# Fused squared-ReLU attention and MLP on one core: q and k transposed from the layout of their loads, and an order of TensorE's work that pulls MLP products forward

## The chip, the cores and the metric

The kernel runs on one core of a Trainium2 chip. A core has TensorE (matrix products), VectorE (DVE), ScalarE (ACT), GpSimd (POOL) and SyncE (SP), which run side by side and wait for each other through semaphores, and 16 DMA engines that all queues share. The metric is the device time of one execution in microseconds (us). The time before is 370.96 us, the median of three runs from 370.91 to 371.25.

## The reference

```python
# q, k, v: (8, 12, 448, 64)    w_in: (768, 2048)    w_out: (2048, 768)
scores = matmul(q, k.transpose(0, 1, 3, 2)) / sqrt(64)
attn = maximum(scores, 0.0) ** 2 / 448
y = matmul(attn, v)                                   # (8, 12, 448, 64)
x = y.transpose(0, 2, 1, 3).reshape(3584, 768)
h = x @ w_in
out = (0.5 * h * (1 + erf(h / sqrt(2)))) @ w_out      # (3584, 768), float32
```

There is no softmax: each score is scaled, clipped at zero and squared. The output of attention goes straight through a two-layer MLP with the exact GELU. The kernel computes in bf16 with float32 accumulation.

## The kernel before, in words

Work goes by batch b = 0 to 7, each of 448 tokens and 12 heads. The heads are taken in G = 3 groups of four. For each group there are seven steps i (`NK`) of attention: QK (`fn_qk`, L686) makes scores of a block of 64 keys for four heads with four matmuls on four 64x64 tiles of the array at once, ACT or DVE clips them into `a_sq` (L698, L700), DVE squares them (L707), and after the seven steps AV (L746) multiplies them with v in 28 matmuls. The result, copied to bf16, is `xT`. F1 (L800) multiplies it with `w_in` in 16 products of six matmuls, ACT applies GELU into `h_sb` (L810), and the second layer multiplies with `w_out`: plainly for the first 256 rows (`add_plain`, L1203), and for groups of 256 rows with seven products in place of eight (Strassen's scheme, `add_group`, L1108). F1 of batches 5 to 7 uses the same scheme (`add_blocks`, L942). Sums of weights that the scheme needs are made by DVE (`tsum` from `w_out`, `wsum` from `w_in`). QK and AV use 64-wide tiles of the array, all MLP products 128-wide ones.

QK needs q and k with the 64 values of a head on the partitions. Natural rows are loaded by GpSimd's queue with a cast to bf16, as `nq` (112 partitions, for each head 4 chunks of 64 values) and `nk` (128 partitions, for each pair of heads 7 chunks of 64). For batches 0 and 1, TensorE transposes them (`add_tk`, `add_tq`). From batch 2 on a DMA transpose on SyncE's queue does it (`add_T_dma`, L632 for kT, L641 for qT). A transpose takes blocks of 128 columns, that is two chunks of 64 at a time: the first lands on partitions 0 to 63, the second on 64 to 127. For QK the two must be chunks that belong together (e = 0 and e = 1 of a pair), so the rows are permuted first into `pq` and `pk`. Batch 2 is permuted by DVE (`permute_k`, `permute_q`), batches 3 to 7 by their loads (`add_wide`: 6 DMAs for k, 12 for q, in runs of 64 values, and one for v).

`add_gate` is a small copy on GpSimd that reads what the last transposes of q write. Since GpSimd works in order, loads that stand behind it in `pool_q` wait until the transposes of that batch have landed. For batch 2 the gate stands ahead of two of the three loads of `w_out` (`add_wout(1)`, `add_wout(2)`).

The order of all instructions is made when the kernel is built. Each piece of work is an `Op` with a fixed duration, and `Scheduler.place` plays the engines forward: first the string `ORDER`, a list of the first pieces by engine and number, then for each engine the piece that can start first by these durations. TensorE's pieces from batch 2 on come from a list of their own, `pe_q`: eight F1 products of batch 1 (`LEAD`), then slots of QK steps, an MLP product or AV in the middle and MLP products between. Loads are modelled at a fixed rate from `DMA_FREE` on, a DMA transpose as 1.2 us of SyncE that lands 3.0 us after its start. On the chip every engine keeps this order and waits where the work isn't ready. Of a batch b + 1 the transposes may not start before a given slot of batch b (`at`).

Of the kernel before, what the change touches and what calls it, by code (L numbers as in the profile page):

```python
# [23 lines left out]
FF = 2048  # L24
KD = DM // 128
# [10 lines left out]
T_TWO = 0.72  # L36
# [8 lines left out]
DMA_FREE = 4.54  # L45
# [11 lines left out]
NEAR = 0.5  # L57
# [4 lines left out]
WIDE = 2.0  # L62
# [13 lines left out]
G0 G1 G2 G3 G4 G5 A10 D13 G6 A16 P11 P14 G7 D12 A15 P17 G8 D18 P21 P39 D22 P33 P36 A34 D40  # L76
P19 D20 A37 P23 G9 P42 P48 D24 P54 A43 D35 A49 P51 D44 P25 D38 A52 D41 G117 A55 D53 P45 D50
A26 D47 A46 P57 D56 P69 P66 A58 D70 P27 G118 A67 P29 D59 P63 G119 A28 D71 P60 A64 G120 D68
P78 D61 A62 P75 A79 D65 P81 P31 D30 A76 D80 P96 G121 D32 A97 P72 D77 G122 A82 D98 P129 G123
D74 A73 P90 D130 P84 P108 A91 G124 D83 P131 A85 D109 P93 P141 D132 A94 D92 P102 D95 P105  # L80
P111 A103 D86 P143 D110 G125 A106 D104 P99 A112 D107 G126 A144 P87 D100 A101 D113 A142 P157
P114 D88 G127 A158 D89 P133 D115 A116 G128 P135 D159 A134 P160 P163 D136 P166 A164 P145 D167
A161 D165 P253 A146 D168 D162 P169 P172 G147 A254 P175 A173 D170 P245 G148 A176 D171 P255
A246 D177 G149 D174 P184 P187 A256 P196 A185 G150 D188 P137 P139 A138 P178 D197 G151 A140
D186 P193 P211 G152 D180 P247 A212 G153 D213 P249 A248 D179 A194 D198 G154 P263 A250 D195
D229 G155 P223 P220 A264 D189 P190 S235 A224 D221 P265 G156 A191 D225 P267 A266 D192 D222
P199 P217 A268 P214 D231 A218 P257 S236 D215 A200 D219 P259 A258 D216 D201 P181 P208 A260
P205 D230 A209 P261 D182 P251 D183 A262 D210 A206 D233 P202 A252 S237 D207 D232 P226 D234
A203 D204 S238 S239 P269
# [17 lines left out]
class Scheduler:  # L107
# [151 lines left out]

    def place(self, fixed):  # L260
# [14 lines left out]
        while rest or any(fixed.values()):  # L275
# [7 lines left out]
            for e, v in fixed.items():  # L283
                if v and not (e == "PE" and by.get("PE")):
                    tops.append(self.pick(v[:1]))
# [11 lines left out]
def kernel(  # L297
# [34 lines left out]
    q32 = natpool.tile([KC, 4, HC * D], F32, tag="pq", name="q32")  # L332
    k32 = natpool.tile([128, 2, NK * D], F32, tag="pk", name="k32")

    def get_nat(b):
        if b not in nq:

            tq, tk = ("pq", "pk") if b == 1 else ("nq", "nk")
            nq[b] = natpool.tile([KC, H, NC * D], BF16, tag=tq, name="nq")
            nk[b] = natpool.tile([128, HP, NK * D], BF16, tag=tk, name="nk")  # L340
            vt[b] = vpool.tile([128, HP, NK * D], BF16, tag="v", name="v_sb")

# [4 lines left out]
    def load_q(b, g0, g1, c0=0, c1=NC):  # L347
        get_nat(b)
        nc.gpsimd.dma_start(  # L349
            nq[b][:, 4 * g0 : 4 * g1, c0 * D : c1 * D], q_view(b, g0, g1, c0, c1)  # L350
        )
# [25 lines left out]
    pqk = []  # L377

    def get_p():
        if not pqk:  # L380
            pqk.append(natpool.tile([KC, NC, DM], BF16, tag="pq", name="pq"))
            pqk.append(natpool.tile([128, G, NK * 128], BF16, tag="pk", name="pk"))
        return pqk

# [3 lines left out]
    def get_T(b):  # L388
        if b not in qkT:
            qkT[b] = (  # L390
                tpool.tile([128, HP, S], BF16, tag="qT", name="qT"),
                tpool.tile([128, G, NK * 128], BF16, tag="kT", name="kT"),
            )
        return qkT[b]

# [24 lines left out]
    Pq, Pk, Tq, Tk = {}, {}, {}, {}  # L420
# [3 lines left out]
    def war(b):  # L424

        old = [o for (bb, *_), o in list(Pq.items()) + list(Pk.items()) if bb == b - 1]
        c = {1: -1, 2: 0}.get(b, b - 1)
        old += [o[0] for (bb, *_), o in list(Tq.items()) + list(Tk.items()) if bb == c]
        return old
# [19 lines left out]
    def add_v(b, g0, g1):  # L449
        def fn():  # L450
            get_nat(b)
            nc.gpsimd.dma_start(vt[b][:, 2 * g0 : 2 * g1], kv_view(v, b, g0, g1))  # L452

        old = [o for (bb, *_), o in AV.items() if bb == b - 3]
        o = dma(fn, (g1 - g0) * 4 * S * 256, old)
        for g in range(g0, g1):
            ld_v[b, g] = [o]

    def add_wide(b):


        def k_fn(e):
            def fn():
                to = get_p()[1].rearrange("p g (i e d) -> e p g i d", e=2, d=D)
                src = kv_view(k, b, 0, G).rearrange("p (g e) (i d) -> e p g i d", e=2, d=D)
                for g in range(G):
                    nc.gpsimd.dma_start(to[e][:, g], src[e][:, g])  # L467

            return fn

        def q_fn(e, j):
            def fn():
                to = get_p()[0].rearrange("p c (g j e d) -> j e g p c d", j=2, e=2, d=D)
                src = q[b].rearrange("(g e j) (p c) d -> j e g p c d", e=2, j=2, c=NC)
                for g in range(G):
                    nc.gpsimd.dma_start(to[j][e][g], src[j][e][g])  # L476

            return fn

        def v_fn():  # L480
            vt[b] = vpool.tile([128, HP, NK * D], BF16, tag="v", name="v_sb")
            nc.gpsimd.dma_start(vt[b], kv_view(v, b, 0, G))

        n = G * 4 * S * 256
        ks = [dma(k_fn(e), WIDE * n / 2, war(b), G) for e in range(2)]
        qs = [dma(q_fn(e, j), WIDE * n / 4, war(b), G) for e in range(2) for j in range(2)]
        old = [o for (bb, *_), o in AV.items() if bb == b - 3]
        o = dma(v_fn, n, old)
        ops = Both(ks), Both(qs)
        for g in range(G):  # L490
            ld_v[b, g] = [o]
            Pk[b, g] = ops[0]
            for c in range(NC):
                Pq[b, g, c] = ops[1]

    class Both:


        def __init__(self, ops):
            self.ops = ops  # L500

        @property
        def done(self):
            ends = [o.done for o in self.ops]
            return None if None in ends else max(ends)

    def add_load(b, g0=0, g1=G):
        if b > 2:
            return add_wide(b)
# [16 lines left out]

    def permute_k(copy, g, src):

        copy(
            get_p()[1][:, g].rearrange("p (i e d) -> p e i d", e=2, d=D),  # L530
            src.rearrange("p e (i d) -> p e i d", d=D),
        )

    def permute_q(copy, g, c0, c1, src):

        dst = get_p()[0][:, c0:c1, 256 * g : 256 * g + 256].rearrange(
            "p c (j e d) -> e p j c d", j=2, d=D
        )
        for e in range(2):
            copy(dst[e], src[:, 2 * e : 2 * e + 2].rearrange("p j (c d) -> p j c d", d=D))  # L540

    def add_pk(b, g0, g1, after=(), bias=0.0):
        for g in range(g0, g1):
            deps = ld_k[b, g] + list(after)
            deps += [Tk[max(b - 1, 1), x, i][0] for x in range(G) for i in range(NK)]
            Pk[b, g] = sch.add(
                (("DVE", 0.31, 0.43),),
                lambda e, g=g: permute_k(V.tensor_copy, g, nk[b][:, 2 * g : 2 * g + 2]), deps,
                bias=bias,
            )  # L550

    def add_pq(b, g0, g1, c0=0, c1=NC, after=(), bias=0.0):
        for g in range(g0, g1):
            deps = [ld_q[b, g, c] for c in range(c0, c1)] + list(after)
            deps += [Tq[max(b - 1, 1), g, c][0] for c in range(c0, c1)]
            if b == 2:
                deps += [Tq[1, x, c][0] for x in range(G) for c in range(NC)]
            d = 2 * (0.07 + (c1 - c0) * 128 / 3840)

            def fn(e, g=g):  # L560
                permute_q(
                    V.tensor_copy, g, c0, c1, nq[b][:, 4 * g : 4 * g + 4, c0 * D : c1 * D]
                )

            op = sch.add((("DVE", d, d + 0.12),), fn, deps, bias=bias)
            for c in range(c0, c1):
                Pq[b, g, c] = op
# [31 lines left out]
    def add_tq(b, g, c0=0, c1=NC, bias=T_BIAS):  # L599
# [14 lines left out]
        def fn2(e):  # L614
            copy(e, get_T(b)[0][:, 2 * g : 2 * g + 2, c0 * KC : c1 * KC], box[0])
# [11 lines left out]
    def add_T_dma(b, after):  # L627

        after = [list(x) for x in after]
        for g in range(G):  # L630
            def fn(e, g=g):
                nc.sync.dma_start_transpose(  # L632
                    get_T(b)[1][:, g].rearrange("p (i t) -> p i t", t=128), get_p()[1][:, g]
                )

            op = sch.add((("SP", 1.2, 3.0),), fn, [Pk[b, g]] + old_T(b) + after.pop(0), mode="X")
            for i in range(NK):
                Tk[b, g, i] = (op, op)
        for c in range(NC):
            def fn(e, c=c):  # L640
# [813 lines left out]
```

## Time and profile before

| | |
|---|---|
| time, median of three | 370.96 us |
| span of the profiled execution | 368.9 us |
| TensorE busy | 358.9 us, 3557 matmuls |
| DVE busy | 288.3 us |
| ACT busy | 200.8 us |
| GpSimd busy | 108.0 us, of it 41.8 for q's loads into `pq` and 28.9 for k's into `pk` |
| DMA packets of GpSimd's loads (q0) | 74992, 58.6% of the time of 16 engines |
| DMA packets of SyncE's queue (q1), transposes and stores | 38768, 26.8% |
| DMA transposes | 18 for kT, 6.8 us to landing (median), 24 for qT, 3.8 us |
| granted TensorE clock | 0.999 |

The profile is one execution. "Busy" of an engine counts its instructions, not what issues DMAs or waits on semaphores. The chain is followed back from the last instruction, at each step to what released it; so its lines tell which work set the end. In a timeline line the numbers are start and duration in us, then engine, line, operation, output and input, count, and in brackets the idle time before with what ended it. "SPq" are DMA issues of SyncE's queue. q0 is the queue that GpSimd's DMAs go through, q1 that of SyncE.

### The profile page before, as it was taken

The numbers are of one execution on the slowest core, as the hardware profiler recorded it, in microseconds if no ns is written. First come the engines' busy times: TensorE is split into PE (matmuls) and PEld (weight loads), VectorE is DVE, ScalarE is ACT, GpSimd is POOL, SyncE is SP. The second block draws the span as 40 slices with busy tenths as digits, with TensorE's granted clock in tenths as the row PEclk, the third lists the DMA queues.
The fourth block names the chain that finished last, engine by engine and source line by source line (L and its number), as shares of the span: only waits on it lengthen the run. The fifth ranks groups of instructions, "written<-read, shape, count | busy, mean of one in ns | idle before, by whom it ended". The sixth has DMA issues, their size and how long they took to land.

```text
span 368.9 us, 8544 instructions
## 1 busy us (share of the span) xinstructions
PE 358.9 (97%) x3557; PEld 222.1 (60%) x3557; DVE 288.3 (78%) x493; ACT 200.8 (54%) x308; POOL 108.0 (29%) x149
## 2 busy tenths in 40 slices
PE   8799999999999999999999999999999999999994
PEld 7566645455544455544455545457886897688663
DVE  2998991789868978987699888888998658665862
ACT  4988865664447845677755588853440353044200
POOL 8666401726087096097095000000000000000000
PEclk9999999999999999999999999999999999999999
DMA  9999999999999999999999960003002301310233
GB/s 174 196 200 204 202 189 134 173 171 131 244 135 167 160 85 172 209 163 154 146 93 133 205 117 2 3 0 87 2 0 88 85 2 29 109 36 2 85 85 88
DMA packets 114166, 42.98 MB, mean 116 GB/s; under 512 B 92816, under 2 KB 110672, under 8 KB 114128
## 3 DMA queue, kind: packets, MB, share of 16 engines
q0 software_dynamic: 74992, 22.47, 58.6%
q1 hardware_dynamic: 38768, 19.46, 26.8%
q8 instruction: 28, 0.46, 0.5%
q10 hardware_dynamic: 368, 0.51, 0.4%
q14 instruction: 10, 0.08, 0.1%
HBM read 45.61 MB, written 11.01 MB: 153 GB/s over the span
## 4 chain that ended last, share of the span: by engine, by line
PE 87%; DMA 4%; DVE 4%; ACT 2%; POOL 1%; issue 1%; DVEq 0%; POOLq 0%; ACTq 0%
PE pso L1108 32%; PE psh L800 24%; PE pb L942 13%; PE ps L686 8%; PE pav L746 6%; PE pso L1203 3%; DMA v_sb<-in_v_dram 2%; DVE a_sq L707 2%; DMA nk<-in_k_dram 2%; ACT a_sq L698 2%; POOL nk L434 0%; POOL v_sb L452 0%; POOL nq L349 0%; PE tp L580 0%; DVE a_sq L700 0%
## 5 line engine op out<-in xcount | busy, mean ns | idle before, releaser
L698 ACT ACTIVATE a_sq<-ps 128x896 bf16<-128x896 f32 (+1 forms) x136 | 117.4, 914 | 44.6 <-PE ps L686 44.5
L707 DVE TENSOR_TENSOR a_sq<-a_sq 128x896 bf16<-128x896 bf16 (+1 forms) x169 | 97.5, 617 | 7.5 <-ACT a_sq L698 7.2
L800 PE MATMUL psh<-xT,win_sb 128*128 128x448 bf16 (+1 forms) x516 | 96.6, 340 | 0.1
L800 PEld LDWEIGHTS <-win_sb 128*128 128x128 bf16 x516 | 47.8, 98 | 45.5 <-issue 10.2
L810 ACT ACTIVATE h_sb<-psh 128x448 bf16<-128x448 f32 x80 | 43.9, 549 | 24.1 <-PE psh L800 23.9
L1108 PEld LDWEIGHTS <-s_sb 128*128 128x128 bf16 x424 | 40.6, 98 | 27.0 <-issue 2.2
L700 DVE TENSOR_SCALAR a_sq<-ps 128x896 bf16<-128x896 f32 x33 | 35.9, 1090 | 18.3 <-PE ps L686 17.8
L686 PE MATMUL ps<-qT,kT 64*64 64x448 bf16 (+1 forms) x756 | 47.3, 336 | 2.2 <-ACT qT L402 0.6
L976 DVE TENSOR_TENSOR part<-pb,part 128x448 f32<-128x448 f32 x60 | 34.6, 619 | 18.4 <-PE pb L942 18.4
L476 POOL DMA_DIRECT2D pq<-in_q_dram x60 | 41.8, 704 | 10.1 <-DVE a_sq L707 6.4
L1108 PEld LDWEIGHTS <-h_sb 128*128 128x128 bf16 x312 | 29.9, 98 | 21.1 <-issue 2.5
L1108 PE MATMUL pso<-wout_sb,s_sb 128*128 128x384 bf16 (+2 forms) x216 | 38.1, 320 | 0.3 <-DVE osb L1142 0.3
L1108 PE MATMUL pso<-wout_sb,h_sb 128*128 128x384 bf16 x208 | 38.1, 326 | 0.0
L1108 PE MATMUL pso<-t_sb,s_sb 128*128 128x384 bf16 x208 | 38.1, 326 | 0.0
L746 PE MATMUL pav<-a_sq,v_sb 64*64 64x448 bf16 (+1 forms) x756 | 36.8, 330 | 0.7 <-ACT a_sq L698 0.4
L686 PEld LDWEIGHTS <-kT 64*64 64x64 bf16 x756 | 18.3, 105 | 24.2 <-issue 17.4
L985 ACT ACTIVATE h_sb<-part 128x448 bf16<-128x448 f32 x36 | 19.8, 578 | 19.9 <-DVE part L976 19.8
L467 POOL DMA_DIRECT2D pk<-in_k_dram x30 | 28.9, 966 | 1.5 <-issue 0.9
L746 PEld LDWEIGHTS <-v_sb 64*64 64x64 bf16 x756 | 21.1, 107 | 13.0 <-issue 2.3
L942 PEld LDWEIGHTS <-win_sb 128*128 128x128 bf16 x288 | 27.6, 98 | 2.2 <-issue 0.4
L1142 DVE TENSOR_TENSOR osb<-pso,p_sb 128x384 f32<-128x384 f32 x39 | 21.7, 556 | 8.2 <-PE pso L1108 5.7
L400 DVE CAST xT<-pav 128x448 bf16<-128x448 f32 (+1 forms) x43 | 23.7, 583 | 4.6 <-PE pav L746 3.9
(62 smaller groups left out, 292.0 us busy)
## 6 DMA issues: line engine op xcount, KB each, us to landing
pk<-in_k_dram POOLq DMA_DIRECT2D x30, 112.0 KB, 4.4
pq<-in_q_dram POOLq DMA_DIRECT2D x60, 56.0 KB, 5.0
v_sb<-in_v_dram POOLq DMA_DIRECT2D x5, 672.0 KB, 9.1
out_dram<-osb SPq DMA_DIRECT2D x8, 336.0 KB, 3.0
wout_sb<-in_moe_w_out_dram POOLq DMA_DIRECT2D x2, 1152.0 KB, 12.1
v_sb<-in_v_dram POOLq DMA_DIRECT2D x9, 224.0 KB, 8.8
out_dram<-osb SPq DMA_DIRECT2D x7, 288.0 KB, 3.4
out_dram<-osb SPq DMA_DIRECT2D x8, 240.0 KB, 3.1
```

The source lines that it names most:

```text
L467: nc.gpsimd.dma_start(to[e][:, g], src[e][:, g])
L476: nc.gpsimd.dma_start(to[j][e][g], src[j][e][g])
L686: nc.tensor.matmul(ps[64 * j : 64 * j + 64, e, x * w : x * w + w], kT[r, g, i * 128 + 64 * j : i * 128 + 64 * j + 64], qT[r, 2 * g + j, co ...
L698: A.activation(ar, ps, AF.Relu, scale=c_att)
L700: V.tensor_scalar(ar, ps, c_att, 0.0, op0=mybir.AluOpType.mult, op1=mybir.AluOpType.max,)
L707: V.tensor_mul(box["a2"][:, :, :used], ar, ar)
L746: nc.tensor.matmul(pav[0][o2 : o2 + 64, e, :w], vt[b][r, 2 * g + e, bass.ts(i, D)], box["a2"][r, e, o : o + w], start=(i == 0), stop=(i == ...
L800: nc.tensor.matmul(ph[:, x * n : x * n + n], win_sb[:, kd, bass.ts(m + x, 128)], xT[b][:, kd, c], start=(kd == 0), stop=(kd == KD - 1),)
L810: A.activation(h_ring()[:, m : m + nm, o + c.start : o + c.stop], box[0][:, :S].rearrange("p (x n) -> p x n", x=nm), AF.Gelu,)
L942: nc.tensor.matmul(bank[name][:, y, z * HS : z * HS + HS], w[:, k, bass.ts(mm, 128)], right()[:, k], start=first and k == 0 and z == 0, st ...
L976: V.tensor_add(get(to), ps(name), get(other))
L1108: nc.tensor.matmul(box[bank][:, n0:n1], left()[:, kf], right[:, kf, n0:n1], start=bool(need) and kf == 0, stop=kf == K2 - 1, skip_group_ch ...
```

## The change

The two transposes read `nq` and `nk` as they were loaded. For k a block of 128 columns holds two neighbouring chunks of the same 14 (two heads of seven chunks), so step i with half e takes chunk 2i + e, which may be of the first or the second head; QK and AV index accordingly. For q all 48 chunks of a batch stand in a row. One transpose of the row gives the even chunks on the lower and the odd on the upper half; a second one that starts 64 columns earlier gives the other parity. Both go into alternating places of a `qT` of 49 slots (`SLOTS`), so that each half of the partitions holds all chunks in order. That takes nine transposes a batch (per group of heads one for k, an even and an odd one for q) in place of seven, no copies, and one load each for q, k and v of batches 3 to 7. Two edge columns of `nq` are set to zero. The gate now waits for all q transposes of its batch, and that of batch 2 moves behind `add_wout(1)` and `add_wout(2)`. The buffers `pq` and `pk` go; natural rows of batch 1, the first float32 rows and sums at the end move to other buffers, and `tsum` tiles are made when first used.

In the planner, `pick_pe` is new: where the next piece of TensorE's list would wait longer than `PULL` (or `PULL_IN` between 64-wide pieces), the next MLP product of the list is taken if it can start sooner. `DMA_FREE`, `NEAR` and the modelled times of a transpose change. `ORDER` is the same list without the six permuting copies (D229 to D234), with the numbers after them shifted by four and its five SyncE entries now the first five of the nine transposes.

```diff
-T_TWO = 0.72
-DMA_FREE = 4.54
+DMA_FREE = 3.05
+SLOTS = H * NC + 1
-NEAR = 0.5
+PULL = 0.15
+PULL_IN = 0.45
+NEAR = 0.25
-WIDE = 2.0
+T_STEP = 1.6
+T_TIME = 4.5
...
+    def pick_pe(self, v):
+        top = self.pick(v[:1])
+        wait = math.inf if top is None else top[1] - self.free["PE"]
+        if v[0].mode == "F" or wait <= (PULL if self.mode == "F" else PULL_IN):
+            return top
+        nxt = next((o for o in v if o.mode == "F"), None)
+        other = nxt and self.pick([nxt])
+        if other and other[1] - self.free["PE"] <= PULL and other[1] < self.free["PE"] + wait:
+            return other
+        return top
...
-                    tops.append(self.pick(v[:1]))
+                    tops.append(self.pick_pe(v) if e == "PE" else self.pick(v[:1]))
...
+                nq[b] = natpool.tile([KC, (H * NC + 2) * D], BF16, tag="nq", name="nq")
+                nk[b] = natpool.tile([128, HP, NK * D], BF16, tag="nk", name="nk")
+                nc.gpsimd.memset(nq[b][:, :D], 0.0)
+                nc.gpsimd.memset(nq[b][:, D + H * NC * D :], 0.0)
...
-                tpool.tile([128, HP, S], BF16, tag="qT", name="qT"),
+                tpool.tile([128, SLOTS * KC], BF16, tag="qT", name="qT"),
...
     def add_load(b, g0=0, g1=G):
-        if b > 2:
-            return add_wide(b)
         add_k(b, g0, g1)
         add_q(b, g0, g1)
         add_v(b, g0, g1)
...
+        def turn(dst, src, deps):
+            return sch.add(
+                (("SP", T_STEP, T_TIME),),
+                lambda e: nc.sync.dma_start_transpose(dst(), src()),
+                deps + old_T(b) + after.pop(0), mode="X",
+            )
+        def slots_of(n, o, k):
+            return lambda: get_T(b)[0].rearrange("p (s t) -> p s t", t=KC)[
+                :, 2 * n + o : 2 * (n + k) + o - 1 : 2
+            ]
+        def q_src(n, o, k):
+            return lambda: nq[b][:, 128 * n + D * o : 128 * (n + k) + D * o]
...
+        n0, odd = 0, None
         for g in range(G):
+            op = turn(k_dst(g), k_src(g), list(ld_k[b, g]))
             for i in range(NK):
                 Tk[b, g, i] = (op, op)
+            lands = list(dict.fromkeys(ld_q[b, g, c] for c in range(NC)))
+            n = 8 * g + 9
+            even = turn(slots_of(8 * g, 1, 8), q_src(8 * g, 1, 8), lands)
+            prior = odd or even
+            beyond = [ld_q[b, g + 1, c] for c in range(NC)] if g < G - 1 else []
+            beyond = list(dict.fromkeys(beyond))
+            odd = turn(slots_of(n0, 0, n - n0), q_src(n0, 0, n - n0), lands + beyond)
+            n0 = n
+            for c, o in enumerate((even, odd, prior, odd)):
+                Tq[b, g, c] = (o, o)
...
-            nc.gpsimd.tensor_copy(gate, get_T(b)[0][:, 0, ::KC])
-        deps = [Tq[b, 0, c][0] for c in range(NC)]
+            nc.gpsimd.tensor_copy(gate, get_T(b)[0][:, ::KC])
+        deps = [Tq[b, g, c][0] for g in range(G) for c in range(NC)]
...
+                            if b < 2:
+                                moving = q_rows(b)[r, 2 * g + j, cols(half)]
+                            else:
+                                n = 4 * (4 * g + 2 * ((2 * i + e) // NK) + j) + 1 - e
+                                moving = qT[r, n * KC : n * KC + S]
...
-            for i, x in enumerate(blocks):
-                _, box, o = SQ[x]
+            for i in range(NK):
...
+                        n, y = (i, e) if b < 2 else divmod(NK * e + i, 2)
+                        _, box, o = SQ[blocks[n]]
...
-                            box["a2"][r, e, o : o + w],
+                            box["a2"][r, y, o : o + w],
...
-    for g in range(G):
-        add_pk(2, g, g + 1, bias=T_TWO)
-        add_pq(2, g, g + 1, bias=T_TWO)
-    add_T_dma(2, [[]] * 7)
-    add_gate(2)
+    add_T_dma(2, [[]] * 9)
     add_wout(1)
     add_wout(2)
+    add_gate(2)
...
-            add_T_dma(b + 1, [at(b, n + (y >= 4)) for y in range(7)])
+            add_T_dma(b + 1, [at(b, n + (y >= 5)) for y in range(9)])
```

## The prediction

> **What bounds the kernel now.** I read the page's busy line first, then who waits for whom on TensorE, then the chain, then the queues of SyncE, GpSimd and the DMA rings around the one place where the change can push on TensorE.
>
> ```profile
> PE 358.9 (97%) x3557; PEld 222.1 (60%) x3557; DVE 288.3 (78%) x493; ACT 200.8 (54%) x308; POOL 108.0 (29%) x149
> ```
>
> TensorE is busy 97% of the span, but the page says that the ends of matmuls are modelled, so I check with cadences from the chain: 80 products of 384 columns in 13.00 us (0.163 us each), 48 of 224 columns in 4.60 us (0.096), 18 of 448 columns in 3.40 us (0.189); QK and AV run four tiles at once, 28 matmuls in 1.32 us. Times the counts of the groups (444 x 0.189 + 72 x 0.096 for F1, 784 x 0.163 for the second layer, 504 x 0.096 for the blocks, 2 x (147 x 0.189 + 42 x 0.096) for QK and AV, some 7 us of transposes and short ones) this is about 337 us of pure streaming. The last matmul ends at 364.3 us, the tail after it is 4.6. Taking each stretch of 10 us as its length less the streaming that starts in it, some 14 us are lost before 30 us (the first loads, then ACT and DVE at 9.4 of 10 us), and only about 11 us from 60 to the end, nearly all of it 0.09 us at each change between 64-wide and 128-wide tiles. The wait list of TensorE from 66 us on has one line:
>
> ```profile
> PE pso L1108 <- DVE osb L1142: 0.3, 1, 0.3
> ```
>
> Matmul starts add four gaps of 0.28 us (152, 203, 233, 244 us) and one of 0.5 at 98 us. So there are 1.6 us to be won by filling TensorE's waits, and any new wait on TensorE after 55 us is paid in full. The chain shows the place to look at:
>
> ```profile
> 54.77 10.32 PE psh L800 x54
> 65.09 0.50 PE ps L686 x8
> ```
>
> The 54 matmuls are the last F1 product of batch 0 and the eight products of batch 1 that `LEAD` puts ahead of batch 2; QK of batch 2 starts straight after them at 65.0. What it needs was ready only just before:
>
> ```profile
> 42.96 11.90 SPq L632 DMA_TRANSPOSE kT<-pk  x3
> 54.96 6.94 SPq L641 DMA_TRANSPOSE qT<-pq  x4
> ```
>
> ```profile
> 63.48 0.19 POOL L653 COPY gate<-qT 128x4 bf16<-128x4 bf16 x1 [19.21 <-DMA qT<-pq]
> 63.71 1.65 POOL L372 DMA_DIRECT2D wout_sb<-in_moe_w_out_dram  x2
> ```
>
> The last DMA transpose landed at 63.4, 1.6 us before use. And GpSimd held two thirds of `w_out` (2 x 1152 KB) back behind the gate until then. The landing times of transposes, first the three of kT issued from 42 to 54 us, beside loads, then the four of qT from 120 to 130 us, with hardly any:
>
> ```profile
> DMA to landing us min/median/max: 8.6/9.8/12.0
> ...
> DMA to landing us min/median/max: 2.7/3.1/4.0
> ```
>
> Why: packets of the two DMA queues (q0 GpSimd's loads, q1 SyncE's transposes; packets, MB, share) in 48 to 50, 50 to 52 and 52 to 54 us, and q1 alone in 60 to 62 us:
>
> ```profile
> q0 software_dynamic: 424, 0.25, 87.8%
> q1 hardware_dynamic: 421, 0.11, 46.2%
> ...
> q0 software_dynamic: 325, 0.29, 94.3%
> q1 hardware_dynamic: 324, 0.08, 37.0%
> ...
> q0 software_dynamic: 225, 0.32, 94.8%
> q1 hardware_dynamic: 226, 0.06, 26.0%
> ...
> q1 hardware_dynamic: 1915, 0.47, 112.8%
> ```
>
> One packet each in turn. A transpose moves 256 B a packet, a load up to 1536 B (`w_out`, 134 ns each), so beside `w_out` transposes get some 112 packets/us, alone 957.
>
> **What the Trainium skill says.** "DMA: Bandwidth & Descriptors", section "Queues, rings and completion order": each DMA engine round-robins between queues at packet granularity; 424 to 421, 325 to 324 and 225 to 226 agree. "TensorEngine Tiling (Array Packing)", "Key Properties": a change of tiling mode drains TensorE; here 0.09 us at each. "TensorE: Matmul & The Clock Gate", Part 1: after an idle window of about 3.4 us TensorE falls to half clock and needs as long to return; no such wait occurs after the start in this trace, so it serves as a bound only.
>
> **The change part by part.**
>
> *No permuted rows, DVE.* Three `pk` copies (385 ns) and six `pq` copies (287 ns) go: 2.9 us of DVE between 42.5 and 53.5 us. TensorE loses about 1 us in 40 to 60 us, its tile changes; it has F1 to run there. Worth 0.
>
> *Loads of batches 3 to 7.* 18 issues with 128-byte packets become one each for k and q: per batch 10752 packets of 32 ns over 16 engines (21.5 us) become 768 of 88 ns and 1344 of 60 ns (9.3 us); GpSimd issues fall from 95 to 15, about 62 of its 108 us. Nobody on TensorE waits for either: batch 3's gate passes at 101.7 and its QK starts at 107.2, batch 4's at 128.9 and 131.5, 5 at 157.2 and 161.4. Worth 0 on the path. The two memsets per batch on GpSimd: at about 0.1 us, 0.
>
> *DMA transposes.* Per batch q has 5488 packets in six transposes (rows of 112 times 8, 9, 8, 8, 8, 8 column blocks) instead of 2688 in four; k keeps 2688. SyncE's time follows from 1.28 us for 768 and 1.36 for 896 columns: nine take 3 x 1.36 + 5 x 1.44 + 1.52 = 12.8 instead of 9.2 us. For batches 3 to 7 this hides: the loads land some 10 us sooner, the cycle is 27 us, and each group of heads needs its own three, not all.
>
> *Batch 2* is the exception, for `add_gate(2)` moves behind `add_wout(1)` and `add_wout(2)`. GpSimd issues these as soon as the queue of eight allows, after landings at 44.3 and 45.6, so they stand right behind `w_out`'s first third (landed 58.1). 1536 more packets of 1536 B then run beside the transposes until about 55.5 + 1640 / 112 = 70 us; in the old kernel the ring was empty of loads from 57 to 64. QK of the first group needs k0 (896 packets), then the even q (896) and the odd q (1008): 2800. The loads of these landed at 42.2, 43.2 and 46.7, so the queue always has work, as before. q1 moved 190, 421, 324 and 226 packets in the stretches from 46 to 54 and 166 to 55.5: 1327. The other 1473 at 112/us take 13.2 us: 68.7, landed at about 69.2. TensorE arrives at 65.0: **a wait of about 4.2 us**. Behind QK in TensorE's fixed order stand the F1 and `w_out` products, then all that follows; ACT and DVE wait for QK's banks. The planner doesn't see it: its transposes land a fixed 4.5 us after issue, which it puts before 55, so the new rule sees nothing to fill. Bounds: 1 us (transposes at 140 packets/us land at 66), 6 us (they land as `w_out` ends, 71). With a wait over 3.4 us the clock may fall: up to 1.7 us more. I take 4.2. The next group needs 2688 more at up to 957/us after 70: 74 to 75 us, in time for 75.0 + 4.2.
>
> *MLP products where TensorE would wait.* At best the 1.6 us of gaps; each product put inside a QK/AV slot costs two tile changes (0.19) against a gap of 0.28. I take 0.4 won.
>
> *QK and AV* have the same matmuls, shapes and counts: 0. The end (products of 250 to 364 us, no loss there): its new buffers wait for QK of batches 6 and 7, done at 217.5 and 247.6, well before use: 0.
>
> Sum: 370.96 + 4.2 - 0.4 = **374.8 us**.
>
> **Rivals.** (1) *Hidden*: batch 2 is in time, because transposes get more turns than I count or the fixed order has other work there; then the gaps are all that moves: 370.96 - 1.0 = 370.0 us. For it: a wait of few us depends on 13 us of one rate. Against: the one-to-one turns. (2) *No difference*: in time, and filled gaps pay for tile changes: 371.0. (3) *Two waits*: half clock after the wait (+1.7), and stores stuck on SyncE. The transposes of batch 3 now wait there for loads behind a gate at about 77 us, so they end near 100; plain stores, at 88 and 92 now, may stand behind them, and the second-layer group after them needs a third and fourth `osb`: +2. 374.8 + 3.5 = 378.3. For it: SyncE's queue is in order; against: that group moves by the same 4 us.
>
> **How the numbers follow.** Wait of batch 2 as computed 0.48; (1) 0.27; (2) 0.14; (3) 0.11. The predicted time is the first. Low end 369.6, a little under (1); high end 377.6, the upper bound of the wait with part of the clock; outside remain most of (3) and the best of (1). Faster 0.27, same 0.14, slower 0.59.
>
> **What would show it.** In the profile after: `w_out` issued near 45 us; q1 at about 110 packets/us until 70 us; a hole in TensorE before the first QK of batch 2, released by a DMA of qT, and none before batches 3 to 7; DVE without `pq`. I am wrong if QK of batch 2 starts at 65, if TensorE's order has more F1 products ahead of it, or if the gain sits before 30 us.

## The result and the profile after

The changed kernel takes **377.77 us** (median of four runs, 377.30 to 378.35) against 371.11 us for the kernel before on the same chip: 1.0176 times as long, 95% interval 1.0155 to 1.0198, so 6.7 us slower. The forecast was 374.8, 3.8 us slower, with a range up to 377.6.

| | before | after |
|---|---|---|
| time, medians on one chip | 371.11 us | 377.77 us |
| GpSimd busy | 108.0 us | 48.2 us |
| packets of GpSimd's loads (q0) | 74992 | 30512 |
| packets of SyncE's queue (q1) | 38768 | 55952 |
| QK of batch 2 starts | 65.0 us | 69.5 us |
| QK of batch 3 starts | 107.2 us | 113.6 us |
| QK of batch 7 starts | 221.3 us | 227.8 us |

The last three rows already say where the time went: 4.5 us ahead of batch 2, 1.9 more on the way to batch 3, and hardly anything after that (6.4 to 6.6 from batch 3 on). The 1.9 us fall into two parts. By the third step of QK (76.67 in place of 70.78) TensorE is 5.9 us late, so 1.4 are lost right behind the first wait; the other 0.5 are lost near 107 us.

The engines' busy times on the page after. TensorE does the same 3557 matmuls, GpSimd less than half of its work:

```profile
PE 359.8 (96%) x3557; PEld 220.7 (59%) x3557; DVE 285.6 (76%) x483; ACT 202.9 (54%) x309; POOL 48.2 (13%) x81
```

TensorE's longest wait, from the list of who waits for whom (total, times, longest), and the same place in its order of work (start, duration, idle time before in brackets):

```profile
PE ps L648 <- DMA qT<-nq: 3.9, 1, 3.9
```

```profile
55.23 10.39 PE L761 MATMUL psh<-xT,win_sb 128*128 128x448 bf16 x54
69.52 0.96 PE L648 MATMUL ps<-qT,kT 64*64 64x448 bf16 x8 [3.90 <-DMA qT<-nq]
70.41 2.32 PE L761 MATMUL psh<-xT,win_sb 128*128 128x448 bf16 x6
```

The same 54 products as before stand ahead of QK (L648). They end at 65.6, and QK, which followed at once, starts at 69.52. Then six products take 2.32 us; later the same six take 1.31. The granted clock says why (stretches of the span; busy time of each engine, then PEclk, DMA share and GB/s):

```profile
65.00:70.00 5.00, 1.10 (x12) 0.32 (x9) 0.96 (x1) 0.61 (x2) 0.00 (x0) 0.91 1.17 203
70.00:72.00 2.00, 2.00 (x13) 0.70 (x6) 1.47 (x2) 0.92 (x1) 0.00 (x0) 0.50 1.23 145
```

By the trace's clock record the clock is at half from 69.08 for 3.41 us. What made QK wait is on GpSimd and in the rings. GpSimd now issues all three thirds of `w_out` at 43.6 to 45.8 us, and the gate passes at 79 instead of 63.5:

```profile
43.56 0.76 POOL L405 DMA_DIRECT2D wout_sb<-in_moe_w_out_dram  x1 [0.35 <-DMA nq<-in_q_dram]
...
45.84 0.82 POOL L405 DMA_DIRECT2D wout_sb<-in_moe_w_out_dram  x1 [0.30 <-DMA nk<-in_k_dram]
...
79.05 0.68 POOL L610 COPY gate<-qT 128x49 bf16<-128x49 bf16 x1 [32.39 <-DMA qT<-nq]
```

The packets of the two queues from 60 to 62 us, where before q1 had the ring to itself and moved 1915, and the times from issue to landing of batch 2's six q transposes:

```profile
q0 software_dynamic: 225, 0.35, 94.2%
q1 hardware_dynamic: 227, 0.06, 22.0%
```

```profile
DMA to landing us min/median/max: 3.1/7.3/22.4
```

One packet each in turn, 225 to 227; so transposes get 113 packets/us beside `w_out` (115 in 64 to 66 us). The third one, the odd half of the first group's q, lands at 69.38.

The second loss is on SyncE and DVE. The chain that ended last, from 81 us on (start, duration, what):

```profile
81.88 9.38 DMA nq<-in_q_dram
...
103.00 0.51 SPq L1036
...
103.56 3.23 DMA out_dram<-osb
...
106.92 0.57 DVE osb L1109
107.53 2.76 PE pso L1075 x16
```

and DVE's wait there:

```profile
DVE osb L1109 <- DMA out_dram<-osb: 1.8, 1, 1.8
```

Two of the plain stores (L1036) go out at 103.0, the other two at 105.5. In the kernel before they went at 87.9 and 92.6, behind the three kT transposes alone:

```profile
83.30 4.49 SPq L632 DMA_TRANSPOSE kT<-pk  x3
87.89 5.44 SPq L1069 DMA_DIRECT2D out_dram<-osb  x4
```

SyncE works in order, and in the new plan eight of the nine transposes of batch 3 stand ahead of the first store. They wait for loads behind the late gate: k's land at 87.8 us, q's at 91.3, and from 91.4 to 102.9 SyncE issues transposes without a pause. The output buffer of the next group comes free at 106.8; DVE waits 1.8 us for it. TensorE, which by its cadence is done at 107.0, loses 0.5 us (its list of waits has 0.3).

### The profile page after: what moved, and what is told of

Same layout as the page of the kernel before. It is cut to its first block, busy times and chain, and to the rows that moved or that the text cites. A ratio compares the mean times of both kernels' runs of the same rounds, so it can differ in the third digit from the quotient of the medians.

```text
span 375.1 us, 8435 instructions
## 1 busy us (share of the span) xinstructions
PE 359.8 (96%) x3557; PEld 220.7 (59%) x3557; DVE 285.6 (76%) x483; ACT 202.9 (54%) x309; POOL 48.2 (13%) x81
## 3 DMA queue, kind: packets, MB, share of 16 engines
q0 software_dynamic: 30512, 22.47, 40.3%
q1 hardware_dynamic: 55952, 23.76, 32.5%
## 4 chain that ended last, share of the span: by engine, by line
PE 74%; SPq 11%; DMA 8%; POOL 2%; DVE 1%; ACT 1%; issue 1%; DVEq 0%; POOLq 0%
PE pso L1075 30%; PE psh L761 18%; PE pb L905 13%; SPq L570 11%; PE ps L648 7%; PE pav L709 6%; DMA nq<-in_q_dram 2%; DMA v_sb<-in_v_dram 2%; DMA nk<-in_k_dram 2%; DMA out_dram<-osb 1%; DMA qT<-nq 1%; ACT a_sq L660 1%; POOL nk L461 1%; DVE part L939 1%; DVE osb L1109 0%
## 5 line engine op out<-in xcount | busy, mean ns | idle before, releaser
L669 DVE TENSOR_TENSOR a_sq<-a_sq 128x896 bf16<-128x896 bf16 (+1 forms) x169 | 98.5, 617 | 8.1 <-ACT a_sq L660 7.2
L761 PE MATMUL psh<-xT,win_sb 128*128 128x448 bf16 (+1 forms) x516 | 98.0, 342 | 0.1
L648 PE MATMUL ps<-qT,kT 64*64 64x448 bf16 (+1 forms) x756 | 47.3, 338 | 5.6 <-DMA qT<-nq 3.9
L662 DVE TENSOR_SCALAR a_sq<-ps 128x896 bf16<-128x896 f32 x32 | 34.8, 1091 | 16.1 <-PE ps L648 15.9
L648 PEld LDWEIGHTS <-kT 64*64 64x64 bf16 x756 | 18.2, 105 | 27.6 <-issue 20.2
L429 DVE CAST xT<-pav 128x448 bf16<-128x448 f32 (+1 forms) x45 | 24.8, 582 | 4.2 <-PE pav L709 2.8
L905 PEld LDWEIGHTS <-ws 128*128 128x128 bf16 x216 | 20.7, 98 | 0.0
L610 POOL COPY gate<-qT 128x49 bf16<-128x49 bf16 x5 | 2.4, 476 | 133.9 <-DMA qT<-nq 133.9
```

The lines of the kernel that those rows point to most:

```text
L429: V.tensor_copy(dst, src)
L648: nc.tensor.matmul(ps[64 * j : 64 * j + 64, e, x * w : x * w + w], kT[r, g, i * 128 + 64 * j : i * 128 + 64 * j + 64], moving, start=True, ...
L662: V.tensor_scalar(ar, ps, c_att, 0.0, op0=mybir.AluOpType.mult, op1=mybir.AluOpType.max,)
L669: V.tensor_mul(box["a2"][:, :, :used], ar, ar)
L761: nc.tensor.matmul(ph[:, x * n : x * n + n], win_sb[:, kd, bass.ts(m + x, 128)], xT[b][:, kd, c], start=(kd == 0), stop=(kd == KD - 1),)
L905: nc.tensor.matmul(bank[name][:, y, z * HS : z * HS + HS], w[:, k, bass.ts(mm, 128)], right()[:, k], start=first and k == 0 and z == 0, st ...
```

## The experiments

**Gate back ahead of `w_out`**, in the changed kernel:

```diff
+    add_gate(2)
     add_wout(1)
     add_wout(2)
-    add_gate(2)
```

> The changed kernel with the gate of batch 2 ahead of the two last loads of w_out again. Theory A (w_out's packets beside the transposes make QK of batch 2 wait): q1 runs alone from 57 us, the odd q of the first group lands near 61, QK of batch 2 starts at 65 to 66 without a hole and without half clock; all nine are down near 67, and w_out lands 12 to 16 us later, near 83, so the plain second-layer products (at 84 in the changed kernel, 78 before) may wait: 371 to 375 us. Theory B (nine transposes are simply too long for SyncE): the hole before QK of batch 2 stays at 3 to 4 us and the time at 377 to 378.

373.84 us, 1.0085 times before [1.0067, 1.0104]. QK of batch 2 starts at 65.13, with no hole and no half clock; the transposes it needs land at 60.8. So turns shared with `w_out` are what held it. But nine transposes end at 67.3 instead of 63.4, so `w_out` lands at 83.25 instead of 79.75, and TensorE's list of waits has two new lines:

```profile
PE ps L648 <- DVE a_sq L662: 1.8, 1, 1.8
PE pso L1170 <- DMA wout_sb<-in_moe_w_out_dram: 1.0, 1, 1.0
```

Those two waits are the 2.8 us (in the first of them DVE stands at a sum of `w_out` whose third lands at 76.8): the gate in the old place costs them elsewhere. Neither of the two places tried for a gate of the whole batch is free.

**The move of the gate alone**, in the kernel before (the three lines of the diff above, the other way round):

> The kernel before, with its own loads, permuting copies and seven transposes, and only the gate of batch 2 moved behind w_out's loads. Theory A (what counts is that move, not the new layout): 5376 packets have to land before QK of batch 2, all four q transposes together: 1327 by 55.5, some 1600 to 70 us, 2450 at 957/us after, landed near 73 to 74: a hole of 8 to 9 us plus half clock, 371.1 + 8.5 + 1.5 = 381 us. Theory C (the new layout's larger transposes are the cause): little change from 371, below 373.

382.31 us, 1.0298 [1.0280, 1.0316], 11.3 us slower. TensorE's list of waits:

```profile
PE ps L686 <- DMA qT<-pq: 9.4, 1, 9.4
```

The clock is at half for 3.7 us of work after it. The move of the gate by itself costs more than the whole change. That the new transposes make it smaller fits their order, though no run changes the order alone: they come group by group and the first group waits for three of nine, whereas the old seven put all of k first, and QK starts only when the last of q has landed (72.7 to 74.5).

**More work ahead of QK of batch 2**: `LEAD = 12` in place of 8, four F1 products that fill the wait.

> The changed kernel with 12 instead of 8 F1 products ahead of batch 2 (4 x 1.14 = 4.6 us). Theory A: the hole of 4.06 us is filled with work that has to be done anyway, the clock stays at full, and both terms vanish: 377.8 - 4.1 - 1.5 = 372.2 us, less up to 0.5 for the wait on a store near 107. Theory B (the loss is a lack of DMA time that moves on to the next group or batch): the time falls by less than 2 us and new holes stand before the second group or batch 3.

378.21 us, 1.0188 [1.0162, 1.0213]: no gain, though QK starts at 69.73 with no idle time. The list of waits:

```profile
PE pso L1075 <- DVE osb L1109: 4.9, 1, 4.9
```

The second wait, 0.5 us in the changed kernel, takes the whole gain: TensorE stops for that output buffer at 99.9 where it came at 107.0, but the first store goes out only 2.6 us sooner (100.4). DVE itself waits 5.6 us for it, and the half clock now follows this wait (104.0 to 107.4).

**Clock kept up** by 17 matmuls on zeros in the wait (added work):

```diff
+FILL = 17
...
+                if blocks[0][:3] == (2, 0, 0):
+                    for _ in range(FILL):
+                        nc.tensor.matmul(
+                            ps[:, 0, :S], zero, win_sb[:, 0, :S], start=True, stop=True
+                        )
```

> The changed kernel with 17 extra matmuls of 448 columns (3.2 us, zero weights, their result overwritten) right ahead of the first QK of batch 2, where TensorE waits. Nothing needs them, so all they change is that TensorE isn't idle. Theory A (the idle time also cost the clock): QK of batch 2 still starts at 69.5, but no stretch at half clock follows: 1.5 us faster than the changed kernel, 376.2 us. Rival (the loss after the hole is something else, such as late operands): the time stays at 377.8.

380.73 us, 1.0273 [1.0253, 1.0293]: slower than without. QK still starts at 69.54, at full clock, and again the store holds TensorE, for 4.3 us at 105.8 with 6.8 us of half clock behind it. In this trace the first store goes out 2.6 us later than in the changed kernel (105.6), behind eight transposes again and with a gate that passes 1.5 us later (80.5); why the gate is late is open. This and the last run showed that the second wait, which I had read as 0.5 us, is a bound of its own.

**Stores first**: transposes of batch 3 start two slots later (`n = {2: 4, 3: 2}` for `{2: 2, 3: 2}` in the plan), so that the plain stores go ahead of most of them.

> The changed kernel with batch 3's transposes planned two slots later (start slot 4 of batch 2 in place of 2), so that on SyncE's queue the two plain stores stand ahead of all but one and three of them. Theory D (two waits in series: first on batch 2's transposes, then on an osb whose store stands behind batch 3's transposes): here the second wait is gone but the first still holds TensorE and its clock up to 72.5 us, and in the changed kernel the second added only 0.5 us: 377.3 us, hole of 4 us before QK of batch 2, none near 107. Rival (the second wait alone sets the time, as the chain through SyncE's queue up to 107 suggests): 372 us.

376.97 us, 1.0158 [1.0142, 1.0174]. The stores go out at 94 and 99, the wait near 107 is gone, the first one stays with its half clock.

**Stores first and clock kept up** (both edits):

> Stores first as in the first kernel of this set, and the 17 extra matmuls that nothing needs where TensorE waits for batch 2. The time up to 69.5 us is the same; what is left out is half clock alone. Theory D: QK of batch 2 at 69.5, full clock, no wait near 107: 377.3 - 1.5 = 375.8 us. If the second wait comes back all the same, 377 or more.

375.19 us, 1.0120 [1.0097, 1.0142]. Full clock throughout, and one delay left, ahead of QK of batch 2 at 69.53, which the added matmuls fill without use.

**Stores first and `LEAD = 12`**:

> The same with 12 F1 products ahead of batch 2. Theory D: both waits are gone, no hole over 1 us after 60 us, full clock: 371.0 to 372.5 us. Rival (time is lost to DMA as such and shows up wherever it is let through): a third hole of some us before QK of batch 3, which starts at 110 or later: 375 or more.

374.03 us, 1.0100 [1.0061, 1.0139]. The wait ahead of batch 2 is filled and none comes near 107 us, but only 2.9 of the 6 us that wait and clock cost come back. QK of batch 7 starts at 222.5 (221.3 before). The profiled run took 377.7 us, the highest of six, and shows a further wait:

```profile
DVE ws L830 <- DMA qT<-nq: 3.7, 1, 3.7
```

The first sum of `w_in` (L830) is written into the buffer of `nq`, which was free by then in the kernel before. Here the last q transpose of batch 7 still reads it and lands at 232.4. Squares stand behind the sum on DVE; TensorE waits three times for DVE, 2.3 us in all between 233 and 238, and the clock is at half from 236.5 to 243.4. The other five runs are 2.1 to 6.1 us above the kernel before; whether they lose it in this place is open, as they have no trace.

**No pull rule** (`PULL` and `PULL_IN` infinite), in the changed kernel, and the **pull rule alone**, in the kernel before:

> The changed kernel with both thresholds of the new rule set to infinity, so that no MLP product is pulled forward. By the fixed order the first product that it moves lies in batch 4's attention, far behind the two waits. All theories: no difference to the changed kernel beyond 0.4 us, 377.4 to 378.2. If the rule costs tile changes it is faster by up to 0.5, if it fills waits slower by as much.

> The kernel before with the rule that pulls an MLP product forward, and nothing else. My prediction gave that rule 0.4 us of gain from TensorE's gaps of 0.28 us. If that holds, 370.6 us or less here. If the rule does nothing that can be measured, 370.6 to 371.4 us, within 0.4 us of the kernel before. A loss of more than 0.4 us would mean that pulled products pay more in changes of tile mode than they fill.

377.38 us without it, where the changed kernel took 377.77, and 370.82 against 371.17 us with it alone, ratio 0.9996 [0.9986, 1.0007], that is between 0.5 us faster and 0.3 slower. No effect of the rule stands out from the noise; a gain of 0.4 us isn't excluded.

**Split gate**: one gate for the first group's q alone ahead of the second third of `w_out`, the full gate ahead of the last. The new gate copies columns 0 to 16 of the 49; the last line sets the order on GpSimd (gate of the first group, second third, full gate, last third):

```diff
+    add_gate(2, 1)
+    w1, w2, gt, first = pool_q[-4:]
+    pool_q[-4:] = [first, w1, gt, w2]
```

> The kernel after with one more gate: a copy of 17 columns of qT on GpSimd, which waits for q's transposes of the first group of heads alone, stands ahead of the second third of w_out; the full gate of batch 2 stands between the second and the last third. If the whole loss comes from transposes of batch 2 sharing turns with w_out and from what follows from that, the first odd q transpose lands near 61 us, QK of batch 2 starts at 65 us with no hole, all transposes of batch 2 land by about 73, the last third of w_out by about 81, and the kernel takes 371 to 372.5 us: as before, with no second wait near 107 us. If the nine transposes themselves, or the unpermuted order of steps, cost something of their own, it stays near 374 as it did with the gate back ahead of both thirds. If w_out's landing set that 374, this kernel is 1.0 us or more under it.

381.42 us, 1.0282 [1.0265, 1.0299]: I had this wrong by 9 us. QK starts at 65.00 as expected, but look at DVE:

```profile
71.79 0.96 DVE L1013 TENSOR_TENSOR t_sb<-wout_sb 128x1536 bf16<-128x1536 bf16 x1 [12.86 <-DMA wout_sb<-in_moe_w_out_dram]
72.66 1.08 DVE L663 TENSOR_SCALAR a_sq<-ps 128x896 bf16<-128x896 f32 x1
```

A sum of `w_out` (L1013) stands ahead of the clipping of QK (L663) and waits for a third that lands at 71.8. By the planner's model that third lands at 62.4 us (72.9 less the 10.5 that a later run adds). Meanwhile no scores are clipped on DVE, and TensorE loses 3.1 us here and 3.9 more at two later places (85.7 and 95.0 us) where it waits for DVE, the first behind a sum of the last third, landed at 83.8. It is the 1.8 us wait of the first experiment over again. The clock adds to the loss: it is at half for 3.41 us after the first of these waits and again after the third (74.9 to 78.3, 98.8 to 102.2).

**Split gate and stores first**:

> The same two gates, and of the transposes of batch 3 all but the first few start two slots later, so that the plain stores go ahead of most of them. If in the split-gate kernel SyncE's queue still holds the stores, this one is 0.5 to 1 us faster than it and near 371; if not, the two agree within 0.4 us. If it comes in below 370.6 the change is worth something once both waits are gone.

381.19 us, 1.0278 [1.0239, 1.0317], the same: the stores weren't what held it.

**Gate for the first group, sums late, stores first**: the gate of the first group stands ahead of both thirds, the full gate goes back behind them, the planner is told of the late landing, so that it puts the sums later, and `n` is as in stores first. Against the split gate:

```diff
-    pool_q[-4:] = [first, w1, gt, w2]
+    pool_q[-4:] = [first, w1, w2, gt]
...
-        ld_wout[i] = dma(lambda: load_wout(kf), DM * 128 * WOUTS[i] * 4)
+        ld_wout[i] = dma(lambda: load_wout(kf), DM * 128 * WOUTS[i] * 4 + 4.1e6 * (i == 1))
```

> The kernel after with three edits. A gate that waits for q's transposes of the first group of heads alone stands ahead of the second and third thirds of w_out, the full gate stays behind both. The planner is told that these thirds land 10.5 us later than it would model (72.9 and 79.0 us), so that DVE's sums of w_out, which stood ahead of clipping and squaring and held both up in the split-gate kernel, come later in DVE's order. And the transposes of batch 3 start two slots later, so that the plain stores go ahead. If the loss of the split-gate kernel is DVE standing at sums whose w_out hasn't landed, and the loss of the kernel after is the shared turns and the stores, then here QK of batch 2 starts at 65 us, w_out lands near 72 and 79, no wait over 1 us follows, and the time is 371 to 373 us. If DVE still waits for w_out it shows as waits of a_sq and the time is 375 or more. Under 370.6 it would mean that the change is worth something by itself.

377.89 us, 1.0183 [1.0155, 1.0210], but for another reason. QK of batch 3 starts at 107.28 (107.19 before) with no wait ahead of it, so both losses of the change are gone. The new one is in batch 4:

```profile
PE pav L710 <- DVE a_sq L670: 3.3, 1, 3.3
```

```profile
DVE osb L1110 <- DMA out_dram<-osb: 4.7, 1, 4.7
```

It is the second wait again, two batches later: stores issued at 148.1, behind a transpose of batch 5 that itself stood until its load landed at 146.7, land at 156.2. DVE holds for the buffer, squares nothing, TensorE stops at AV, and the clock is at half for 6.8 us behind it (157.1 to 163.9).

**That one removed too**: transposes of batch 5 start two slots later (`n = {2: 4, 3: 2, 4: 3}`).

> The last kernel with one more edit: the transposes of batch 5 start two slots later, behind the two pairs of stores of batch 4. In the last kernel QK of batch 3 started at 107.3 us, as in the kernel before, with no wait on TensorE behind it; then the first transpose of batch 5 stood on SyncE from its load's landing at 146.8, the stores behind it landed at 156.2, and DVE waited 4.7 us for their osb, TensorE 3.3 us for DVE, with half clock after it. If the three waits (turns shared with w_out, stores behind transposes of batch 3, stores behind transposes of batch 5) are all that the change costs, this kernel takes 370.5 to 372 us, QK of batch 5 starts at 161 to 162 us. If the nine transposes cost more than that, a further wait shows at QK of batch 5 or later and the time stays over 373. Under 370.5 would mean that the change is worth something by itself.

373.31 us, 1.0069 [1.0042, 1.0096]; its runs spread from 372.01 to 375.49. The profiled one is that of 372.01, with QK of batches 3, 4 and 5 at 107.3, 131.6 and 161.7 us (107.2, 131.5, 161.4 before), clock 0.998, and one wait over 1 us:

```profile
PE ps L649 <- DMA qT<-nq: 1.2, 1, 1.2
```

That is QK of batch 6 at 192.3, whose transposes now come late in their turn. DVE's list has the sum of `w_in` again:

```profile
DVE ws L831 <- DMA qT<-nq: 1.2, 1, 1.2
```

TensorE loses nothing to it in this execution. Up to 161 us the profiled run is level with the kernel before, so there the new transposes and loads can be had for nothing. The median doesn't show that for the whole kernel: at 373.3 us and with a wait at batch 6, it falls to the side of the expectation on which the nine transposes cost more than the three waits.

## Why the prediction was right in kind and short in size

*The first wait: right.* The step said that 1473 packets at 112/us would land the first group's q at 69.2 and TensorE, arriving at 65.0, would wait 4.2 us. Measured: 113 packets/us, landing at 69.38, QK 4.5 us late. The one-to-one turns that "DMA: Bandwidth & Descriptors", section "Queues, rings and completion order", states decided it, and the trace before already had them. With the gate back the wait is gone.

*The clock: this step failed.* "With a wait over 3.4 us the clock may fall: up to 1.7 us more. I take 4.2." I worked out a wait that was longer than 3.4 us and then set its consequence to nothing. The clock fell, for 3.41 us, and cost 1.4 us by the timeline, 1.8 by the pair of kernels with stores first (376.97 without the fill, 375.19 with it). "TensorE: Matmul & The Clock Gate", Part 1, has the window at about 3.4 us, and the length of the pieces agrees. Its condition of an idle window doesn't hold strictly here: the clock fell after waits of 2.1 to 3.35 us too (last section). The 1.7 belonged in the sum.

*The second wait: wrongly left to a rival of 0.11.* The rival named the place: stores stuck on SyncE behind transposes of batch 3, the group after them short of a third and fourth `osb`. Against it I set that "that group moves by the same 4 us". But the store it waited for moved by 15 us (88.7 to 103.6), the group by some 6. The rival as a whole, half clock and store, stood at 378.3, nearest to the 377.8 measured. The cost of the store in the changed kernel is 0.5 us by the timeline, 0.8 by runs (377.77 less 376.97), less than the 2 I gave, but only because the first wait hides most of it: with `LEAD = 12` it is 4.9.

*The pull rule: 0.4 us of gain that no run shows* (377.38 without it, 377.77 with it; 370.82 with it alone, 371.17 before), and that none excludes.

The sum in place of mine, read from the timeline: 4.5 for the wait, 1.4 for the clock, 0.5 for the store: 6.4, measured 6.7. The medians give 4.3 (375.19 less 370.93), 1.8 and 0.8; these three differences add up to the loss by their construction, so they divide it and don't confirm it. The rivals "hidden" and "no difference" fell with QK at 69.5.

*Two more steps that were wrong, though they cost little in this kernel.* The loads of batches 3 to 7 don't "land some 10 us sooner": q's last lands at 91.3, 122.8, 148.1, 180.0 and 205.8 us, in the kernel before at 94.6, 122.1, 149.8, 176.6 and 203.9. They take less time (14 us in place of 20 from the first issue to the last landing for batch 4), but are issued later (108.6 in place of 102.2 us for batch 4, 195.9 in place of 184.0 for batch 7), behind gates that wait for the last of nine transposes. So the margin on which "this hides" rested wasn't there. And the end's "new buffers" wait not only for QK but for the last q transpose of batch 7, which reads `nq`. It lands at 227.3 us (216.5 before) and the sum starts at 233.9, so the changed kernel has room; with `LEAD = 12` and stores first it hasn't.

*What cost nothing, as said:* DVE without the permuting copies and 60 us less work on GpSimd, as far as the last kernel's trace shows, which is level with the kernel before up to 161 us. The nine transposes did cost: with the gate ahead of `w_out` 2.8 us by way of `w_out`'s landing (I didn't ask what stood behind the gate), and in other kernels by way of the stores behind them.

*Open:* why the last kernel's other runs are up to 3.5 us above its profiled one, and whether later transposes of batches 6 and 7 would bring it to the time before. The planner's changed constants (`DMA_FREE`, `NEAR`, the modelled times of a transpose) were not run alone. No version of the change beat the kernel before.

## What to carry to other kernels

When a change moves one transfer, follow both in-order queues it passes through to their next consumers: here a gate that moved 16 us on GpSimd came back 24 us later as a store on SyncE and again as an output buffer on DVE. A wait that is short in the profile may be short because an earlier wait hides it, so removing the earlier one alone gains nothing; price the second as if the first were gone. And if you compute a wait of some 2.5 us or more of TensorE, put the half clock into the sum, not into the range: in these traces every such wait was followed by it.

## What the runs showed of the hardware that was not expected

- A store of 32 rows of 3072 B took 8.1 us to land behind a DMA transpose of its own queue that shared turns with loads (issued 148.1, landed 156.2; the transpose ahead of it landed at 156.0); a store of 112 such rows with no loads beside it took 3.2 (166.1 to 169.3). Both are of the kernel with late sums.
- Half clock came in pieces of 3.41 us or whole multiples of it, and the length of the wait did not settle how many. One piece followed waits of 3.9 us (changed kernel), 4.0 (stores first), 4.7 (no pull rule), 4.9 (`LEAD = 12`), 3.0 and 2.1 (split gate) and 2.4 (split gate and stores first); two pieces followed 4.3 (the fill alone), 3.35 (late sums) and three short waits of 2.3 in all (stores first and `LEAD = 12`); three followed the 9.4 of the moved gate. None followed single waits of 1.0 to 1.8 us, nor one of 2.1 at 96.6 us (split gate and stores first). So the cost of a wait of given length varied by a factor of two.
